# A fused attention and adapter kernel: PSUM as one pool of banks, single-group output, a chosen engine for each eviction, a finer last batch, and a listed order

## The chip, the cores and the metric

One Trainium2 chip, of which the kernel uses one core. The metric is device microseconds (us) of one launch; lower is better.

## The reference

The reference takes q, k and v of shape (8, 8, 576, 64) (batch, heads, sequence, head size) and three weight arrays. It computes attention within a window of 32 positions to each side, joins the 8 heads to rows of 512, and adds to each row a mixture of two of eight rank-16 adapters:

```python
scores = scale * np.matmul(q, k.transpose(0, 1, 3, 2))
mask = np.abs(pos[:, None] - pos[None, :]) <= window          # window = 32
scores = np.where(mask, scores, -1000000000.0)
attn = softmax(scores)                                        # over the last axis
x = np.matmul(attn, v)  ->  rows (4608, 512)
logits = x @ w_gate                                           # 8 experts
topk = np.argpartition(-logits, K, axis=1)[:, :K]             # K = 2
w = softmax of the two chosen logits
delta[mask] += w[mask, k, None] * ((x[mask] @ A[e]) @ B[e])   # for each chosen expert e
return x + delta
```

## The kernel before, in words

The kernel cuts the work into small tasks with two- or three-letter names and numbers. There are 8 batches (b) of 4 units; a unit (u, 0 to 31) is a pair of heads. Queries and keys are loaded as 18 tiles (t) of 128 folded rows; scores are made in 36 tiles (T), two for each t. Each task runs on one engine:

- POOL issues the loads: LD.t.w (line 272; w is 0 for q, 1 for k) and LV.b.o (line 279, v, two halves). It also makes the constants.
- DVE regroups a loaded tile (RG.t.w, line 288), shifts half of v (SV.b.o, line 284), divides the attention output by its row sums (MU.u, lines 355 and 356), evicts transposed rows (XE.b.h, line 374) and computes the gates (G1.b, lines 399 to 404, and G2.b, lines 414 to 420). At the start it clears buffers (ZK, ZV, ZP).
- PE transposes q and k (TR.t.w, line 296, 8 matmuls), makes scores (SC.T, lines 323 and 327, 2 + 8 matmuls), attention times v (PV.u, line 346, 13 matmuls), transposes of the result (TX.b.h, line 368), the projections to adapters and logits (PZ.b, line 382, 20 matmuls), transposes of the gated projections (TZ.b, line 427) and the output (PD.b.h, lines 437 and 440: for each group of 128 rows one matmul of 512 columns for the adapters and four of 128 for the rows themselves).
- ACT evicts transposed keys in two halves (EK.t, line 316), evicts queries for odd t (EQ.t, line 305; even t go to DVE), takes the exponentials (EX.T, line 332) and one small exponential for the gates (GA.b, line 407), and evicts TZ (ZE.b, line 431) and the output (OB.b.h, line 449).
- SP issues the stores (ST.b.h, line 457).

In SBUF a whole tile of q or k is 256 KB, and a half of v for one batch 288 KB. A batch has 5 groups of 128 output rows; h = 0, 1, 2 stands for groups 0 and 1, 2 and 3, and 4.

PSUM is held as three tiles of two banks (W, 1024 float32 columns, for SC, PV, PZ and PD) and two tiles of one bank (T, 1024 float16 columns, for TR, TX and TZ):

```python
Ws = [psum.tile([128, 1024], F32, name=f"W{i}") for i in range(NW)]    # NW = 3
Ts = [psum.tile([128, 1024], F16, name=f"T{i}") for i in range(NTP)]   # NTP = 2
```

The function `plan` sets the order. It gives each task an engine, a cost and a due time, and places the tasks one after the other on engines and PSUM tiles; the kernel then issues them in that order. The order is thus fixed at build time, and each engine works off its own tasks in order. Semaphores between the engines are set by the framework, which looks at what tile each instruction reads and writes.

Of the kernel before, what the change touches and what calls it, by code (L numbers as in the profile page):

```python
# [38 lines left out]
NT = NU * NB // TB  # L39
NV, NPT, NRAW, NCAST, NX, NXT, NOB = 3, 4, 6, 3, 2, 2, 3  # L40
NW, NTP = 3, 2
# [8 lines left out]
class Task:  # L50
    __slots__ = ("key", "eng", "cost", "deps", "take", "give", "due", "start", "end",
                 "left", "users", "ready", "slot", "lat", "seq")

    def __init__(self, key, eng, cost, deps, take=None, give=None, lat=0.2):
        self.key, self.eng, self.cost, self.deps = key, eng, cost, deps
        self.take, self.give, self.lat = take, give, lat


OFF = {"LD": -14.73, "LV": -10.97, "RG": -16.63, "TR": -2.72, "EQ": -37.15, "EK": 25.79, "SV": 12.6,
       "SC": -0.11, "EX": 11.83, "PV": 1.3, "MU": -33.19, "TX": 3.53, "XE": -49.66, "PZ": 7.11,  # L60
       "G1": -57.49, "GA": 7.42, "G2": -66.76, "TZ": -23.09, "ZE": 10.68, "PD": 11.21, "OB": 13.67,
       "ZK": 4.21, "ZV": 30.71, "ZP": 29.46}


def tasks(off=OFF):

    ts = {}

    def add(key, u, eng, cost, deps, take=None, give=None, lat=0.2):
        t = Task(key, eng, cost, deps, take, give, lat)  # L70
        t.due = u + off[key[0]]
        t.seq = len(ts)
        ts[key] = t

    def score_tiles(u):
        return range(NB * u // TB, (NB * u + NB - 1) // TB + 1)

    def units(T):
        return [u for u in range(NU) if T in score_tiles(u)]

    for i in range(NR):
        add(("ZK", i), BT * i / NB - 4, "DVE", 1.25, [])
    for i in range(NPT):
        add(("ZP", i), -3.0 + i, "DVE", 0.56, [])
    for i in range(NV):
        for o in (0, 1):
            add(("ZV", i, o), 4 * i, "ACT" if i == 1 else "DVE", 2.2 if i == 1 else 1.2, [])
    for t in range(NTT):
        u = BT * t / NB
        for w in (0, 1):  # L90
            add(("LD", t, w), u, "DMA", 1.5, [("RG", t - NRAW, w)], lat=2.0)
        for w in (0, 1):
            add(("RG", t, w), u, "DVE", 0.43, [("LD", t, w), ("TR", t - NCAST, w)])
        old = [("SC", 2 * (t - NR) + i) for i in (0, 1, 2)]
        for w in (0, 1):
            add(("TR", t, w), u, "PE", 0.46, [("RG", t, w)] + old, take="T")
        wrap = 0.2 if t % NR in (0, NR - 1) else 0.0
        add(("EQ", t), u, *(("ACT", 1.02 + wrap) if t % 2 else ("DVE", 0.69 + wrap)),
            [("TR", t, 0)], give=("TR", t, 0))
        add(("EK", t), u, "ACT", 2.05, [("TR", t, 1), ("ZK", t % NR)], give=("TR", t, 1))  # L100
    for b in range(B):
        for o in (0, 1):
            add(("LV", b, o), NP * b + o, "DMA", 1.8,
                [("PV", NP * (b - NV) + n) for n in range(NP)], lat=2.0)
            add(("SV", b, o), NP * b, "DVE", 0.78, [("LV", b, o)])
    for T in range(NT):
        t = T // 2
        need = [("EQ", t), ("EK", t)]
        if T % 2 and (TB * T + TB - 1) % NB != NB - 1:
            need.append(("EQ", t + 1))  # L110
        need += [("PV", u) for u in (units(T - NPT) if T >= NPT else [])]
        add(("SC", T), TB * T / NB, "PE", 0.90, need, take="W")
        add(("EX", T), TB * T / NB, "ACT", 1.03, [("SC", T)], give=("SC", T))
    for u in range(NU):
        b = u // NP
        add(("PV", u), u, "PE", 0.80,
            [x for T in score_tiles(u) for x in (("EX", T), ("ZP", T % NPT))]
            + [(k, i, o) for k, i in (("SV", b), ("ZV", b % NV)) for o in (0, 1)]
            + [("TX", b - NX, h) for h in range(3)], take="W")
        add(("MU", u), u, "DVE", 1.05, [("PV", u)], give=("PV", u))  # L120
    off["ST"] = off["OB"]
    for b in range(B):
        v0 = NP * b
# [100 lines left out]
def kernel(  # L224
# [291 lines left out]
    for t in order:  # L516
# [40 lines left out]
```

## Time and profile before

| | |
|---|---|
| time, 3 runs | 145.54, 145.97, 146.17 us (median 145.97) |
| the profiled execution's own time | 147.01 us |
| its span, first to last instruction | 145.0 us |
| PE busy | 119.1 us, 1624 matmuls |
| DVE busy | 109.9 us |
| ACT busy | 111.0 us |
| mean granted TensorE clock | 0.973 |

The profile page has the busy time of each engine, the span in 40 equal slices (a digit is the busy share in tenths; PEclk is the granted clock), the chain of work that ended last, and groups of equal instructions with their mean time and the idle time before them. Other answers of the trace list the waits by pairs of lines, and the instructions in order of time. A row of the chain in order of time reads: start, length, engine, tile, line, count. A row of the timeline reads: start, length, engine, line, operation, output from input, count, and in brackets the idle time before it and what ended it.

### The profile page before, as it was taken

Reading aid. Unit: us, or ns where it says so; the run is one execution under the profiler, and the core shown is the slowest. Engines: PE = TensorE matmul, PEld = TensorE weight load, DVE = VectorE, ACT = ScalarE, POOL = GpSimd, SP = SyncE. Lnnn points to the kernel's source line nnn. Section 1 sums busy time; section 2 is a strip of 40 time slices with the busy share of each in tenths; the row PEclk is TensorE's granted clock in tenths of the full one; section 3 lists DMA queues with packets and bytes.
Section 4 is the critical chain, followed back from the end, with each engine's and each line's share of the span. In section 5 each row is a group of like instructions: output and inputs, shape, how many; then the busy total and the mean of one; then the engine's idle time right before and its main releaser. Section 6 shows DMA issues by size and latency. Waiting matters only on the chain.

```text
span 145.0 us, 4013 instructions
## 1 busy us (share of the span) xinstructions
PE 119.1 (82%) x1624; PEld 100.9 (70%) x1624; DVE 109.9 (76%) x279; ACT 111.0 (77%) x127; POOL 52.0 (36%) x80
## 2 busy tenths in 40 slices
PE   0257959796789599999999999999999999792770
PEld 0246757685677598888979788988898788582440
DVE  5769889993895989899899999989778456946000
ACT  7739877569769569999998999889979975553160
POOL 7998377589534355546256021000000000000000
PEclk9999999999999999999999999999999999999558
DMA  2999999999999999999999999924403050548035
GB/s 10 204 141 183 199 198 188 132 128 142 163 195 180 190 243 207 198 283 229 223 209 276 195 216 280 178 58 156 133 0 127 16 188 5 192 136 300 28 127 199
DMA packets 38770, 24.12 MB, mean 166 GB/s; under 512 B 24800, under 2 KB 34144, under 8 KB 38752
## 3 DMA queue, kind: packets, MB, share of 16 engines
q0 software_dynamic: 33504, 14.43, 84.1%
q1 hardware_dynamic: 5248, 9.44, 19.0%
q8 instruction: 12, 0.20, 0.5%
q14 instruction: 6, 0.05, 0.1%
HBM read 28.85 MB, written 9.44 MB: 264 GB/s over the span
## 4 chain that ended last, share of the span: by engine, by line
PE 51%; DVE 24%; issue 10%; DMA 8%; ACT 2%; POOL 1%; ACTq 0%; DVEq 0%; POOLq 0%
PE W L346 10%; DMA l<-in_q_dram 8%; PE W L323 7%; PE W L327 7%; PE T L296 6%; PE W L437 5%; PE W L382 5%; PE W L440 5%; PE T L368 4%; DVE x L356 4%; DVE c L288 4%; DVE vbd L284 3%; DVE xT L374 3%; DVE rc L355 2%; DVE zs L420 2%
## 5 line engine op out<-in xcount | busy, mean ns | idle before, releaser
L316 ACT COPY kR<-T 64x1024 f16<-64x1024 f16 x36 | 36.2, 1005 | 7.1 <-PE T L296 6.8
L332 ACT ACTIVATE PT<-W 128x1024 f16<-128x1024 f32 x36 | 35.4, 1038 | 5.5 <-PE W L327 4.6
L346 PE MATMUL W<-vbd,PT 128*128 128x130 f16 x416 | 28.6, 219 | 2.0 <-DVE vbd L284 2.0
L296 PE MATMUL T<-ident,c 128*128 128x128 f16 x288 | 22.6, 229 | 9.0 <-DVE c L288 7.7
L449 ACT COPY ob<-W 128x1024 f32<-128x1024 f32 (+1 forms) x24 | 20.9, 876 | 9.9 <-PE W L440 7.7
L356 DVE TENSOR_TENSOR x<-W,rc 128x640 f16<-128x640 f32 x32 | 26.4, 824 | 1.1
L346 PEld LDWEIGHTS <-PT 128*128 128x128 f16 x416 | 25.0, 97 | 2.3 <-DVE vbd L284 2.3
L327 PEld LDWEIGHTS <-kR 128*128 128x128 f16 x288 | 19.5, 99 | 8.9 <-issue 0.7
L296 PEld LDWEIGHTS <-c 128*128 128x128 f16 x288 | 18.7, 103 | 9.7 <-DVE c L288 9.6
L323 PE MATMUL W<-identQ,mask 128*128 128x512 f16 x72 | 22.0, 387 | 2.7 <-DVE x L356 2.7
L327 PE MATMUL W<-qR,kR 128*128 128x128 f16 x288 | 22.4, 222 | 0.0
L272 POOL DMA_DIRECT2D l<-in_k_dram x24 | 15.9, 665 | 10.5 <-DMA l<-in_k_dram 3.1
L279 POOL DMA_DIRECT2D vbd<-in_v_dram x16 | 13.3, 835 | 16.0 <-PE T L427 7.4
L272 POOL DMA_DIRECT2D l<-in_q_dram x24 | 16.4, 683 | 7.0 <-DMA l<-in_k_dram 1.9
L288 DVE COPY c<-l 128x1024 f16<-128x1024 f16 x36 | 14.6, 434 | 5.4 <-DMA l<-in_k_dram 4.5
L440 PEld LDWEIGHTS <-xT 128*128 128x128 f16 x160 | 13.3, 104 | 7.1 <-issue 2.8
L437 PE MATMUL W<-B_sb,zT 128*128 128x512 f16 x40 | 16.4, 410 | 1.8 <-ACT zT L431 0.8
L374 DVE COPY xT<-T 128x1024 f16<-128x1024 f16 (+1 forms) x24 | 13.4, 598 | 4.6 <-PE T L368 3.8
L440 PE MATMUL W<-ident,xT 128*128 128x128 f16 x160 | 16.7, 231 | 0.0
L368 PE MATMUL T<-ident,x 128*128 128x128 f16 x160 | 11.8, 219 | 3.0 <-DVE xT L374 1.5
L284 DVE COPY vbd<-vbd 32x2304 f16<-32x2304 f16 x16 | 12.7, 794 | 0.7 <-DMA vbd<-in_v_dram 0.3
L368 PEld LDWEIGHTS <-x 128*128 128x128 f16 x160 | 9.8, 98 | 3.6 <-DVE x L356 1.7
(49 smaller groups left out, 115.5 us busy)
## 6 DMA issues: line engine op xcount, KB each, us to landing
out_dram<-ob SPq DMA_DIRECT2D x24, 256.0 KB, 2.9
vbd<-in_v_dram POOLq DMA_DIRECT2D x16, 288.0 KB, 9.4
l<-in_q_dram POOLq DMA_DIRECT2D x12, 256.0 KB, 9.6
l<-in_k_dram POOLq DMA_DIRECT2D x12, 256.0 KB, 9.9
out_dram<-ob SPq DMA_DIRECT2D x16, 192.0 KB, 2.9
l<-in_q_dram POOLq DMA_DIRECT2D x4, 192.0 KB, 7.6
l<-in_k_dram POOLq DMA_DIRECT2D x4, 192.0 KB, 7.3
l<-in_q_dram POOLq DMA_DIRECT2D x4, 128.0 KB, 9.1
```

Source lines behind the costliest of these rows:

```text
L272: keep(nc.gpsimd.dma_start(out=raw[w][t % NRAW][f - FT * t:f - FT * t + n], in_=src[f - NF * b:f - NF * b + n]))
L296: keep(nc.tensor.matmul(out=tp[:, FT * slot:FT * slot + FT], lhsT=src[:, j, :], rhs=ident, is_transpose=True, start=True, stop=True))
L316: keep(nc.scalar.copy(out=dst.rearrange("p a (r f j) -> p a r f j", r=2, j=4), in_=kt[64 * o:64 * o + 64]))
L323: keep(nc.tensor.matmul(out=p[:, i:i + 4], lhsT=maskT, rhs=bcast(identQ, 1, 4), start=True, stop=False))
L327: keep(nc.tensor.matmul(out=p[:, i], lhsT=kR[:, a, :], rhs=qR[:, :, 8 * a:8 * a + 16], start=False, stop=(i % 4 == 3)))
L332: keep(nc.scalar.activation(out=PTs[T % NPT][:, :, 64:192].rearrange("p i (f j) -> p i f j", j=J), in_=ps("SC", T).rearrange("p (i j f) -> ...
L346: keep(nc.tensor.matmul(out=po[:, GS * g:GS * g + 2 * VD], lhsT=PTs[T % NPT][:, sl, off:off + 128], rhs=rhs[:, :, V0 - 1:V0 + D], start=(i ...
L356: keep(nc.vector.tensor_tensor(out=xs[b % NX].rearrange("p g (h n d) -> p g h n d", h=2, n=NP)[:, :, :, n], in0=pog[:, :, :, 1:VD], in1=bc ...
L368: keep(nc.tensor.matmul(out=tp[:, c0:c0 + 128], lhsT=xs[b % NX][:, g, 128 * c:128 * c + 128], rhs=ident, is_transpose=True, start=True, st ...
L437: keep(nc.tensor.matmul(out=pd[:, i], lhsT=zTs[b % 2][:, g], rhs=B_sb, start=True, stop=False))
L440: keep(nc.tensor.matmul(out=pd[:, i, 128 * c:128 * c + 128], lhsT=xTs[b % NXT][:, g, c], rhs=ident, start=False, stop=(c == 3)))
L449: keep(nc.scalar.copy(out=dst, in_=src))
```

## The change

- The eight PSUM banks are held as four tiles W0 to W3 of two banks. A task that needs two banks (SC, PV, PZ) takes a tile; a task that needs one takes one half of a tile, which it views as float16 where it holds transposes. The number behind the colon in the list below is the bank: banks 2i and 2i + 1 are the halves of Wi.
- The output is made, evicted and stored by single groups (PD.b.g, OB.b.g, ST.b.g), with 7 buffers of one group instead of 3 of two groups.
- Each eviction has an engine of its own in the list (A for ACT, D for DVE): EK's two halves apart (34 on A, 2 on D), EQ 11 on A and 7 on D, XE 7 on A and 19 on D, OB 30 on A and 10 on D.
- In the last batch TX and XE go by single groups; MU.31 is MA and MB, PZ.7 is PZa and PZb, G2, TZ and ZE have two parts too; and the rows' part of the output (PX) is issued ahead of the gates, and the adapters' part (PB) behind them.
- One comparison of G2 moves into G1. The identity is made ahead of the first load; the mask, the weights' loads and the cleared columns (CQ, CM, WA, WB, Z1) are entries of the list. NRAW goes from 6 to 4, NXT from 2 to 3.
- `Task`, `tasks` and `plan` are gone: the order, the banks and the engines stand in a list.

```diff
-NT = NU * NB // TB
-NV, NPT, NRAW, NCAST, NX, NXT, NOB = 3, 4, 6, 3, 2, 2, 3
-NW, NTP = 3, 2
+NV, NPT, NRAW, NCAST, NX, NXT, NOB = 3, 4, 4, 3, 2, 3, 7
+NW = 4
+LB = B - 1
...
+ORDER = """
+CI ZK.1 LD.0.0 LD.0.1 ZK.2 LD.1.0 ZV.1.0:A ZP.2 LD.1.1 ZP.1 WB ZK.0 ZV.2.0:A CQ RG.0.0 CM
+ZV.0.1:D TR.0.0:0 LV.0.0 RG.0.1 LD.2.0 ZK.3 EQ.0:A TR.0.1:1 RG.1.0 LD.2.1 EK.0.0:A RG.1.1
+TR.1.0:0 Z1.2 Z1.1 ZP.3 EK.0.1:A TR.1.1:2 LD.3.0 EQ.1:D LD.3.1 EK.1.1:A SC.0:4 ZP.0 LV.0.1
+ZV.2.1:D EK.1.0:A LD.4.0 SC.1:0 ZV.0.0:D EX.0 LD.4.1 SC.2:2 RG.2.0 EX.1 RG.2.1 LV.1.0 ZK.4
+TR.2.0:4 EX.2 TR.2.1:5 WA RG.3.0 EQ.2:A Z1.0 ZV.1.1:D TR.3.0:2 EQ.3:A SC.3:0 RG.3.1 SV.0.0
+EK.2.0:A TR.3.1:4 SV.0.1 LV.1.1 EX.3 EK.3.0:D PV.1:2 LD.5.0 EK.2.1:A PV.2:0 LD.5.1 MU.1 EK.3.1:A
+PV.0:6 LD.6.0 MU.2 SC.4:2 LD.6.1 MU.0 SC.5:4 EX.4 SC.6:0 LV.2.0 RG.4.0 EX.5 RG.4.1 LV.2.1 PV.3:2
+SV.1.0 EX.6 TR.4.1:4 LD.7.0 MU.3 TR.4.0:5 LV.3.1 EK.4.1:A TX.0.1:2 LD.7.1 EQ.4:A SV.1.1 TX.0.0:3
+LD.8.0 TX.0.2:0 XE.0.1:D PV.4:6 LD.8.1 XE.0.2:A RG.5.0 LV.3.0 EK.4.0:A SC.7:0 MU.4 LD.9.0
+TR.5.0:2 XE.0.0:D EX.7 PV.5:6 RG.5.1 SC.8:4 EQ.5:A MU.5 LD.9.1 PZ.0:0 EX.8 RG.6.0 RG.6.1 LD.10.0
+TR.5.1:6 G1.0 TR.6.1:7 LD.10.1 EK.5.0:A PV.6:4 SV.2.0 SC.9:2 GA.0 EK.5.1:A G2.0 EX.9 TR.6.0:6
+EQ.6:A MU.6 TZ.0:0 PV.7:2 ZE.0:A RG.7.0 SC.10:4 LV.4.1 MU.7 EK.6.1:A SC.11:0 LD.11.0 SV.3.1
+EX.10 TX.1.0:6 RG.7.1 TX.1.2:2 LV.4.0 TX.1.1:3 EX.11 XE.1.0:D TR.7.1:4 LD.11.1 XE.1.1:D TR.7.0:5
+EK.6.0:A PD.0.1:6 RG.8.0 PD.0.0:3 XE.1.2:D EQ.7:A LD.12.0 SC.12:0 RG.8.1 SV.2.1 LD.12.1 OB.0.1:A
+TR.8.0:2 SV.3.0 EX.12 TR.8.1:5 ST.0.1.1 PV.9:6 EQ.8:D OB.0.0:A PV.8:0 MU.9 EK.8.0:A ST.0.0.0
+PZ.1:2 MU.8 EK.7.1:A SC.13:6 EK.7.0:A G1.1 PV.10:0 EX.13 RG.10.0 PD.0.4:4 MU.10 GA.1 SC.15:6
+OB.0.4:A G2.1 EK.8.1:A ST.0.4.4 PV.11:0 EX.15 PD.0.3:4 LV.5.1 PD.0.2:5 MU.11 TZ.1:2 OB.0.3:A
+LV.5.0 SC.14:6 ZE.1:A RG.9.1 ST.0.3.3 TX.2.2:4 RG.9.0 EX.14 TX.2.1:0 RG.10.1 LD.13.0 TX.2.0:1
+XE.2.1:D TR.9.1:2 XE.2.2:A PV.12:6 XE.2.0:D EK.9.0:A LD.13.1 RG.11.1 TR.9.0:4 MU.12 PD.1.0:3
+OB.0.2:A LD.14.0 PV.13:0 EQ.9:A ST.0.2.2 RG.12.0 LD.14.1 TR.10.1:6 MU.13 TR.10.0:7 OB.1.0:A
+SC.16:4 EK.9.1:A ST.1.0.5 RG.12.1 RG.11.0 PZ.2:0 EX.16 SV.4.1 LD.15.0 EQ.10:D SC.17:2 EK.10.1:A
+LD.15.1 G1.2 PV.14:4 EX.17 PD.1.1:7 LD.16.0 MU.14 OB.1.1:A PV.15:2 LD.16.1 GA.2 ST.1.1.6
+EK.10.0:A PD.1.4:7 G2.2 LV.6.1 SC.19:4 OB.1.4:A LV.6.0 PD.1.2:6 EX.19 ST.1.4.9 PD.1.3:7 MU.15
+TZ.2:0 TR.11.1:1 OB.1.2:A RG.13.0 SC.20:4 ZE.2:A ST.1.2.7 RG.14.1 LD.17.0 OB.1.3:A RG.13.1
+TX.3.2:6 TX.3.0:0 XE.3.2:D EX.20 LD.17.1 ST.1.3.8 TX.3.1:7 XE.3.0:D SC.18:2 EK.11.1:A XE.3.1:D
+TR.11.0:0 SV.4.0 TR.12.0:7 EX.18 TR.12.1:6 RG.15.0 PV.17:4 EQ.11:A EQ.12:D PV.16:2 MU.17
+EK.11.0:A PD.2.4:0 PD.2.0:7 MU.16 OB.2.4:A SC.23:4 EK.12.1:A ST.2.4.14 OB.2.0:D SC.21:0 EX.23
+RG.15.1 ST.2.0.10 PZ.3:2 RG.14.0 SV.5.0 EX.21 SC.22:4 G1.3 EK.12.0:A PV.18:0 SV.5.1 EX.22
+SC.24:6 MU.18 GA.3 PV.19:4 EX.24 G2.3 PD.2.3:0 LV.7.1 TR.13.0:1 OB.2.3:A PD.2.1:6 LV.7.0 EQ.13:A
+TR.13.1:7 ST.2.3.13 MU.19 TZ.3:2 TR.14.0:3 OB.2.1:A SC.25:0 RG.16.1 ZE.3:A ST.2.1.11 EQ.14:D
+EK.13.1:A TX.4.1:6 TX.4.2:2 RG.17.0 TX.4.0:4 XE.4.2:D EX.25 PD.3.0:5 XE.4.0:D PV.20:2 OB.3.0:A
+XE.4.1:D TR.14.1:4 EK.13.0:A ST.3.0.15 MU.20 PD.2.2:5 PV.21:0 OB.2.2:A SV.7.0 PZ.4:6 EK.14.1:A
+ST.2.2.12 MU.21 EK.14.0:A PD.3.1:5 SC.26:2 G1.4 OB.3.1:A PV.22:0 EX.26 ST.3.1.16 RG.16.0 SC.27:4
+RG.17.1 GA.4 MU.22 TR.16.0:2 EX.27 TR.15.0:3 G2.4 PV.23:0 EQ.15:A PD.3.4:4 TR.15.1:5 MU.23
+OB.3.4:A TZ.4:6 PD.3.2:3 EK.15.0:A ST.3.4.19 PD.3.3:4 EQ.16:D TX.5.1:7 OB.3.2:A SV.6.0 TX.5.0:0
+ZE.4:A ST.3.2.17 TX.5.2:1 SC.28:2 XE.5.0:D OB.3.3:A XE.5.2:D EK.15.1:A PD.4.3:6 ST.3.3.18
+XE.5.1:D PD.4.2:4 SC.29:0 EX.28 SV.6.1 OB.4.2:D TR.16.1:7 EX.29 PV.24:2 SV.7.1 ST.4.2.22 PZ.5:4
+EK.16.0:A MU.24 EK.16.1:A PV.25:0 G1.5 SC.30:2 OB.4.3:A MU.25 ST.4.3.23 GA.5 SC.31:6 EX.30 G2.5
+TR.17.0:0 EX.31 PV.26:2 TR.17.1:1 MU.26 TZ.5:4 EK.17.0:A PV.27:6 EQ.17:D PD.4.4:5 ZE.5:A SC.32:2
+MU.27 PD.5.0:4 EX.32 OB.4.4:D TX.6.2:0 TX.6.0:6 XE.6.2:D TX.6.1:7 ST.4.4.24 XE.6.0:A OB.5.0:D
+SC.33:2 EK.17.1:D ST.5.0.25 XE.6.1:A PV.28:4 PD.4.1:0 EX.33 MU.28 PZ.6:6 OB.4.1:A PV.29:4 G1.6
+ST.4.1.21 SC.34:0 MU.29 GA.6 SC.35:2 EX.34 G2.6 PD.4.0:4 EX.35 PV.30:0 PD.5.1:5 OB.4.0:A MU.30
+PV.31:2 OB.5.1:A ST.4.0.20 TZ.6:4 ST.5.1.26 MA.31 PD.5.4:5 ZE.6:A PD.5.3:0 MB.31 TX.7.0:1
+TX.7.1:4 OB.5.3:D XE.7.0:A TX.7.4:2 TX.7.2:3 TX.7.3:6 XE.7.1:D XE.7.2:A PD.6.0:7 ST.5.3.28
+XE.7.4:D PD.6.1:4 XE.7.3:A OB.5.4:D PZa.7:2 OB.6.1:A ST.5.4.29 PZb.7 OB.6.0:A ST.6.1.31 PD.6.2:4
+G1.7 ST.6.0.30 PD.5.2:5 OB.6.2:A PX.7.0:6 ST.6.2.32 PD.6.3:4 OB.5.2:D GA.7 PX.7.1:0 G2a.7
+ST.5.2.27 G2b.7 TZa.7:5 OB.6.3:D ZEa.7:A TZb.7:2 ZEb.7:A PB.7.0 ST.6.3.33 PB.7.1 OB.7.0:A
+OB.7.1:D PX.7.2:2 PB.7.2 OB.7.2:A ST.7.0.99 OB.7.3:A ST.7.1.99 OB.7.4:D ST.7.2.99 ST.7.3.99
+ST.7.4.99 PD.6.4:2 OB.6.4:A ST.6.4.34
+"""
...
-    ts, order = plan()
+    order, where = [], {}
+    for word in ORDER.split():
...
     def ps(*key):
-        t = ts[key]
-        return (Ws if t.take == "W" else Ts)[t.slot]
+        return Ws[int(where[key]) // 2]
+
+    def bank(*key):
+        i = int(where[key])
+        return Ws[i // 2][:, 512 * (i % 2):512 * (i % 2) + 512]
+
+    def bank16(*key):
+        return bank(*key).bitcast(F16)
+
+    def copy_on(*key):
+        return nc.scalar.copy if where[key] == "A" else nc.vector.tensor_copy
...
+    def MA(u):
+        recip(u)
+        mult(u, 0, 3)
+
+    def MB(u):
+        mult(u, 3, NG)
...
+    def gs(b, h):
+        return range(h, h + 1) if b == LB else range(2 * h, min(NG, 2 * h + 2))
...
+    def resid(b, g, pd, first):
+        for c in range(4):
+            keep(nc.tensor.matmul(out=pd[:, 128 * c:128 * c + 128], lhsT=xTs[b % NXT][:, g, c],
+                                  rhs=ident, start=(first and c == 0),
+                                  stop=(not first and c == 3)))
+
+    def PD(b, g):
+        delta(b, g, bank("PD", b, g), start=True, stop=False)
+        resid(b, g, bank("PD", b, g), False)
...
+    def PX(b, h):
+        for g in range(2 * h, min(NG, 2 * h + 2)):
+            resid(b, g, half(b, g), True)
+
+    def PB(b, h):
+        for g in range(2 * h, min(NG, 2 * h + 2)):
+            delta(b, g, half(b, g), start=False, stop=True)
+
+    def OB(b, g):
+        src = half(b, g) if b == LB else bank("PD", b, g)
+        keep(copy_on("OB", b, g)(out=obs[(NG * b + g) % NOB], in_=src))
...
```

365 lines of the change are left out of this document (112 added, 253 removed).

## The prediction

> **What bounds the kernel now.** I read the page's slices first, then the chain in order of time, then the timeline of the two ends and the groups of equal instructions.
>
> ```profile
> span 145.0 us, 4013 instructions
> PE   0257959796789599999999999999999999792770
> DVE  5769889993895989899899999989778456946000
> ACT  7739877569769569999998999889979975553160
> PEclk9999999999999999999999999999999999999558
> GB/s 10 204 141 183 199 198 188 132 128 142 163 195 180 190 243 207 198 283 229 223 209 276 195 216 280 178 58 156 133 0 127 16 188 5 192 136 300 28 127 199
> ```
>
> PE is full from slice 14 (51 us) to slice 34 (127 us). Ahead of that it has holes, behind it holes and half the clock. DVE and ACT are not far behind PE in the middle. What one task costs PE at full clock stands in the chain, where the starts follow each other without a hole:
>
> ```profile
> 65.40 0.43 PE W L323 x2
> 65.83 0.45 PE W L327 x8
> 66.28 0.45 PE T L296 x8
> 66.73 1.18 PE W L382 x20
> 67.91 0.75 PE W L346 x13
> ...
> 74.70 0.28 PE T L427 x5
> ...
> 88.13 0.89 PE T L368 x16
> ...
> 89.90 0.23 PE T L368 x4
> ...
> 108.12 0.22 PE W L440 x4
> 108.56 0.22 PE W L440 x4
> ```
>
> So SC is 0.88, TR 0.45, PZ 1.18, PV 0.75, TZ 0.28, TX of a batch 1.12, and an output group 0.44 (from one start to the next). All of it: 36 x 0.45 + 36 x 0.88 + 32 x 0.75 + 8 x (1.12 + 1.18 + 0.28) + 40 x 0.44 = 110.1 us. The span is 35 us longer: that is the head, the tail, and little else. Three places on the timeline cut it up:
>
> ```profile
> 5.81 0.77 PEld L296 LDWEIGHTS <-c 128*128 128x128 f16 x8 [5.81 <-DVE c L288]
> 12.42 1.06 PE L323 MATMUL W<-identQ,mask 128*128 128x512 f16 x2
> 18.87 0.81 DVE L284 COPY vbd<-vbd 32x2304 f16<-32x2304 f16 x1
> 19.74 1.67 PE L346 MATMUL W<-vbd,PT 128*128 128x130 f16 x26 [1.79 <-DVE vbd L284]
> 28.54 0.59 PE L323 MATMUL W<-identQ,mask 128*128 128x512 f16 x2
> 36.52 0.59 PE L323 MATMUL W<-identQ,mask 128*128 128x512 f16 x2 [1.64 <-DVE x L356]
> 49.22 0.91 PE L346 MATMUL W<-vbd,PT 128*128 128x130 f16 x13
> 124.19 0.91 PE L346 MATMUL W<-vbd,PT 128*128 128x130 f16 x13
> 131.20 0.20 DVE L399 TENSOR_REDUCE m<-W 128x5 f32<-128x40 f32 x1 [1.64 <-PE W L382]
> 133.54 0.82 DVE L420 TENSOR_TENSOR zs<-W,gate 128x640 f16<-128x640 f32 x1
> 134.43 0.71 PE L427 MATMUL T<-ident,zs 128*128 128x128 f16 x5 [2.82 <-DVE zs L420]
> 139.60 1.50 ACT L449 COPY ob<-W 128x1024 f32<-128x1024 f32 x2 [0.69 <-PE W L440]
> ```
>
> The row at 49.22 is PV.8. Counted along PE's instructions, 15 TR, 13 SC, 9 PV, two TX, one PZ, one TZ and two output groups are done at its end (49.97): 29.5 us of work, 20.5 lost. The row at 124.19 is PV.31, the last; behind it stand 11 output groups, two TZ, one TX and one PZ, 7.7 us. Between the two, 110.1 - 29.5 - 7.7 = 72.9 us of work take 75.1 us: the middle loses 2.2. The tail takes 145.0 - 125.1 = 19.9 us.
>
> **The change: what each edit costs its engine.**
>
> ```profile
> L316 ACT COPY kR<-T 64x1024 f16<-64x1024 f16 x36 | 36.2, 1005 | 7.1 <-PE T L296 6.8
> L332 ACT ACTIVATE PT<-W 128x1024 f16<-128x1024 f32 x36 | 35.4, 1038 | 5.5 <-PE W L327 4.6 <-DVE rc L355 0.7
> L356 DVE TENSOR_TENSOR x<-W,rc 128x640 f16<-128x640 f32 x32 | 26.4, 824 | 1.1
> L288 DVE COPY c<-l 128x1024 f16<-128x1024 f16 x36 | 14.6, 434 | 5.4 <-DMA l<-in_k_dram 4.5 <-DMA l<-in_q_dram 0.7
> L449 ACT COPY ob<-W 128x1024 f32<-128x1024 f32 x16 | 16.3, 1016 | 8.5 <-PE W L440 6.3 <-issue 1.1 <-ACT kR L316 0.8
> L374 DVE COPY xT<-T 128x1024 f16<-128x1024 f16 x16 | 10.5, 688 | 4.1 <-PE T L368 3.4 <-ACT ob L449 0.5
> L305 ACT COPY qR<-T 128x1024 f16<-128x1024 f16 x9 | 9.1, 1014 | 2.6 <-PE T L296 2.4
> L431 ACT COPY zT<-T 128x640 f16<-128x640 f16 x8 | 5.6, 695 | 2.7 <-PE T L427 2.6
> L449 ACT COPY ob<-W 128x512 f32<-128x512 f32 x8 | 4.8, 596 | 1.4 <-PE W L440 1.3
> ```
>
> Single groups: 40 copies instead of 24. Thirty on ACT are 30 x 0.596 = 17.9 us where 16.3 + 4.8 = 21.1 were; ten go to DVE. A 512-column float32 copy on DVE is in no row: between 0.34 (half of the 688 ns, float16) and 0.82 (640 columns of float32); I take 0.65, from the nearer float32 row. DVE gets 6.5 us. ACT in turn gets two more EQ (2 us), five large-batch XE and two small (5 us) and loses two EK. So ACT and DVE each carry some 3 to 5 us more in all; PE's 110.1 us stay. SP issues 40 stores as before, and the store buffers hold slightly more: nothing. NRAW from 6 to 4 costs nothing as long as a tile is regrouped 10 us before the tile four later is needed; in the walk below RG.8.0 frees its buffer at 46 for a tile used at 62.
>
> **The change: the waits.** The built program shows what the list doesn't say. Bank numbers are free, but the semaphores are set by tile, and a tile is now a pair of banks that different tasks hold. Two places, in the order of the built program:
>
> ```
> PE   18 L189 Matmult W_103<-ident,c_0_84 128x128 [waits Activation_49]
> DVE 274 L414 TensorCopy ob_97<-W_106 128x512 [waits DMAHW4_49,Activation_49]
> ```
>
> The first is TR.0.1 into bank 1: it waits for ACT's copies of EQ.0 out of bank 0. The second is OB.7.1 on DVE, which waits for OB.7.0 on ACT, two reads of different banks. Some hundred instructions wait like this, among them PE in front of nearly every single output group, and ACT and DVE for each other. So I walked the list by hand, each engine in its order, with the durations above, these waits, and 0.05 us for a semaphore.
>
> ```profile
> 3.51 0.23 POOL masks.py:197 MEMSET ident<- 128x128 f16 x1
> 3.81 0.29 POOL masks.py:199 TENSOR_SCALAR_AFFINE_SELECT ident<-ident 128x128 f16<-128x128 f16 x1
> ```
>
> *Head.* The identity is made ahead of the first load (these two rows, some 0.6 us), so TR.0.0 starts at 6.4. EQ.0 ends at 8.65, and only then TR.0.1 may start; EK.0.0 ends at 10.75, TR.1.0 (bank 0) at 11.8, EK.0.1 (bank 1) behind it at 12.85. SC.0 starts at 12.9, before at 12.42. The second half of v for batch 0 is now loaded behind tile 3: 2.8 MB instead of 2.1 MB. Before, its shift began at 18.87 and PV at 19.74; the 0.7 MB more take 3.6 us at the 198 GB/s of slice 6. If the loads came strictly one after the other, it would land near 18.8 even so (the first five slices, 18.1 us, moved 2.7 MB). I take 21.5, nearer to the first since that is counted from a landing, and PV starts at 22.3. In between PE has scores and transposes of tiles 2 and 3 to do, and bank pairs give room for three scores at once: SC.6 is done at 28 (before it began at 28.54 and took 0.88). From there DMA, DVE and these waits carry it to the end of SC.12 at 47.9. The same set of tasks was done before at 49.97 - 0.75 (PV.8) + 0.45 (TR.7.1) = 49.7. **Head: -1.8 us.**
>
> *Middle.* Up to PV.31 the list now has 101.5 us of PE work (13 output groups come behind it, before 11), less 29.2 done, that is 72.3. In the walk PE stops here: for an OB or EK of the other bank, or a chain through one, in front of PZ.1 (0.6), PD.0.4 and PD.0.3 (0.4), PD.1.1 and PD.1.4 (1.45), TX.3.2 and TX.3.1 (0.65), TR.11.0 (0.5), TX.4.1 (1.4), TR.14.1 (0.7), PD.3.1 (0.85), PD.3.3 (0.95) and PD.4.2 (0.3), in all 7.8; for other work in front of SC.15, PV.15 and PD.2.3, 1.6; small change 0.9. That is 10.3 us where 2.2 were lost. PV.31 ends at 47.9 + 72.3 + 10.3 = 130.5, before 125.1. Against the head's gain that is **middle: +7.2 us** (0.6 less work, 8.1 more waiting, rounded with the steps).
>
> A typical step: EQ.14 (DVE, bank 3) waits for ZE.3 (ACT, bank 2), EK.13.1 stands behind ZE.3 on ACT, TX.4.1 (bank 6) waits for EK.13.1 (bank 7) and PE stands still from 90.3 to 91.7.
>
> *Tail.* From the end of PV.31: MA 0.85 and MB 0.45, by columns from the 824 ns; five TX and five XE, the XE in turn on ACT and DVE, done at +4.4; PZa and PZb at +5.5; the gates' first part at +6.8 (both parts took from 131.20 to 134.4 before, and take as long in themselves). OB.5.2 (DVE) stands ahead of the second part and waits for PD.6.3 in the other bank, so the second part starts at +8.1 and ends at +10.2; TZa and ZEa, behind OB.6.3, at +11.4; PB and the last five OB up to +14.3. From the last copy's end to the end of the span it is 145.0 - 141.1 = 3.9 us as before. In all 18.2 instead of 19.9. **Tail: -1.7 us.** What helps is that the rows' part of the output no longer stands behind the gates: before, ten matmul steps at half the clock followed ZE.
>
> On the clock: PE idles 2.0 us behind PX in the walk. In the trace 2.82 us idle were followed by five transposes in 0.71 instead of 0.28; a shorter idle than that, of 1.64 us, was followed by full speed. Between the two I take full clock; at half it is up to 1.3 us more. The Trainium skill, "TensorE: Matmul & The Clock Gate", Part 1, has the clock fall after an idle window of about 3.4 us; by that nothing is added here, though the measured fall came after less.
>
> **Sum.** 145.0 - 1.8 + 7.2 - 1.7 = 148.7 us of span; with the 2.0 us around it 150.7 against the profiled 147.01. That execution lies 1.0 above the median of the runs; on the median the same 3.7 us give 149.6. I say 149.5 us.
>
> **Rivals.** *The pair waits bite little: faster.* Most of the middle's stops are shorter than one eviction (0.6 to 1.0 us); if the evictions come up on their queues one place earlier than in the walk, they vanish. With waits by bank alone, the middle loses 3 instead of 10.3, the head gains 3.5 (then the loads of tiles 7 and 8, at 44 to 47 us, end last), the tail 4.9 (OB.5.2, OB.6.3 and OB.7.1 wait no more) and 0.9 of output work moves behind PV.31 into holes: 145.97 - 3.5 + 0.2 - 4.9 = 138. For it: PSUM by banks would let two tasks share a pair. Against it: the waits stand in the built program. The Trainium skill, "PSUM — Partial Sum Buffer", PSUM bank collisions, asks only that two engines keep apart by bank and quadrant; by that rule none of the pair waits is needed by the chip, and the time would be this rival's. It decides if the middle's loss stays below 5 us. Chance 0.23.
>
> *Half the price: level.* The middle at +3.6 instead of +7.2 eats the ends' 3.5: 146. Chance 0.11.
>
> *DVE becomes the bound: slower yet.* DVE's middle, by the rows, is 23 MU, 21 RG, six gates, 12 XE, ten SV, seven EQ or EK and four OB, some 70 us beside PE's 72.3, and it now waits for ACT and is waited for. If it, not PE, ends last through the middle, add 3 us: 152.6. For it: DVE was at nine tenths in most middle slices. Against: before, it ended few waits of PE there. Chance 0.16.
>
> *The change does not do what it says* is part of the forecast: the banks are pooled by number, not in the waits.
>
> **How the numbers follow.** The forecast (slower by 2 to 6 us) has 0.50. What a measurement can tell from no change is about 0.5%, 0.7 us. Faster: 0.23 and 0.02 from the level case, 0.25. Same: 0.07 of the level case. Slower: the rest, 0.68. The likeliest case alone spans 147.5 to 152. The range for all reaches down to 141 (the upper part of the faster rival) and up to 154 (DVE as bound with the half clock in the tail).
>
> **What would show it.** Right: waits of PE for lines 208 and 414 (EK, OB) of half a microsecond and more in the middle, in front of lines 388, 189 and 278; SC.0 near 13 us; the end of PV.31 (last matmul of line 238) near 130; a tail near 18. Wrong: PE full from 40 us on with PV.31 near 118, or SC.12 done before 45. If the middle is as lossy as said and the time is still lower, the tail or the head was mis-sized.

## The result and the profile after

The changed kernel takes 153.3 us (median of 4 runs, 152.66 to 153.88), the kernel before beside it 145.75 us (4 runs, 145.33 to 146.17): 1.052 times as long, 95% interval 1.046 to 1.057. The forecast was 149.5 us, in a range of 141 to 154. The direction is right, and the size is half of what was measured: 3.5 us forecast, 7.5 measured. The profiled execution took 153.19 us. Where some runs of a kernel lie more than 1.5% above its fastest, the median without these upper runs is given below beside the median of all, and the ratios to the kernel before always leave them out.

The page's span and slices:

```profile
span 151.4 us, 4024 instructions
PE   0239648989798899997899987879799999886560
DVE  6876889988995988998577994788699897856430
ACT  8658785898898699987987967877888685662250
PEclk9999999999999999999999999999999999999555
```

PE, full before from 51 to 123 us, now has sevens and eights all through the middle, while DVE and ACT are no fuller. PE and ACT work hardly more (120.6 us for 119.1, 111.9 for 111.0), DVE 6.6 us more (116.5 for 109.9), and everybody waits more. At the end the granted clock is at half for three slices. The timeline has the marks that the forecast named, and some of the stops it listed:

```profile
8.88 1.01 PE L189 MATMUL W<-ident,c 128*128 128x128 f16 x8 [1.19 <-ACT qR L200]
12.65 1.06 PE L215 MATMUL W<-identQ,mask 128*128 128x512 f16 x2
48.21 0.61 PE L219 MATMUL W<-qR,kR 128*128 128x128 f16 x8
92.68 1.28 PE L278 MATMUL W<-ident,x 128*128 128x128 f16 x20 [1.08 <-ACT kR L208]
95.79 0.61 PE L189 MATMUL W<-ident,c 128*128 128x128 f16 x8 [0.65 <-ACT ob L414]
99.56 0.38 PE L388 MATMUL W<-B_sb,zT 128*128 128x512 f16 x1 [0.79 <-ACT kR L208]
106.81 0.38 PE L388 MATMUL W<-B_sb,zT 128*128 128x512 f16 x1 [0.90 <-ACT kR L208]
129.83 0.91 PE L238 MATMUL W<-vbd,PT 128*128 128x130 f16 x13
```

The first row is TR.0.1, which waits until ACT has emptied the other bank of its pair; SC.0 follows at 12.65. SC.12 is done at 48.7 (start of its last eight matmuls plus 0.45), PV.31 at 130.7. Called head up to the end of SC.12, middle up to the end of PV.31, and tail behind it, the head is 1.0 us shorter than before (48.7 for 49.7), the middle 6.6 longer (82.0 for 75.4), the tail 0.8 longer (20.7 for 19.9): 6.4 us, the difference of the spans. The four rows between are TX.4.1, TR.14.1, PD.3.1 and PD.3.3. Each waits for an EK or OB (lines 208, 414) in the other bank. The waits by pairs of lines have them together:

```profile
PE W L388 <- ACT kR L208: 3.2, 5, 0.9
PE W L189 <- ACT kR L208: 3.0, 4, 1.1
PE W L189 <- ACT qR L200: 1.2, 1, 1.2
PE W L278 <- ACT kR L208: 1.1, 1, 1.1
```

(Columns: microseconds in all, times, longest.) The copies themselves cost what was assumed; the ones on DVE took 0.689 us where 0.65 was guessed:

```profile
L414 ACT COPY ob<-W 128x512 f32<-128x512 f32 x30 | 17.3, 588 | 11.5 <-PE W L392 4.1 <-DVE xT L284 1.5 <-PE W L189 1.3
L414 DVE COPY ob<-W 128x512 f32<-128x512 f32 x10 | 6.9, 689 | 5.7 <-ACT ob L414 2.3 <-PE W L392 1.2 <-ACT kR L208 0.8
```

The tail, from the timeline:

```profile
138.60 0.69 DVE L414 COPY ob<-W 128x512 f32<-128x512 f32 x1 [0.98 <-PE W L392]
140.79 0.72 PE L362 MATMUL W<-ident,zs 128*128 128x128 f16 x5 [1.78 <-DVE zs L343]
142.11 0.75 ACT L366 COPY zT<-W 128x384 f16<-128x384 f16 x2 [4.08 <-DVE ob L414]
142.64 1.89 PE L388 MATMUL W<-B_sb,zT 128*128 128x512 f16 x4 [1.13 <-ACT zT L366]
144.33 0.69 DVE L414 COPY ob<-W 128x512 f32<-128x512 f32 x1 [2.31 <-ACT ob L414]
146.16 0.58 PE L388 MATMUL W<-B_sb,zT 128*128 128x512 f16 x1 [0.78 <-DVE ob L414]
147.21 0.58 ACT L414 COPY ob<-W 128x512 f32<-128x512 f32 x1 [1.53 <-PE W L392]
```

OB.5.2 on DVE (138.60) waits for PE (PD.6.3 in the other bank) and holds the gates' second part. PE stands for 1.78 us, and its five transposes then make a row of 0.72 us, where such a row is 0.44 long at full clock (TZ.6, at 131.15). ZEa waits for OB.6.3 on DVE in the other bank, and OB.7.1 for OB.7.0 in the other bank. PD.6.4 waits for OB.7.4, but that is no pair wait: both use bank 2.

### The profile page after: what moved, and what is told of

Its sections match the earlier page's. It is cut to its first block, busy times and chain, and to the rows that moved or that the text cites. A ratio compares the mean times of both kernels' runs of the same rounds, so it can differ in the third digit from the quotient of the medians.

```text
span 151.4 us, 4024 instructions
## 1 busy us (share of the span) xinstructions
PE 120.6 (80%) x1624; PEld 100.6 (66%) x1624; DVE 116.5 (77%) x284; ACT 111.9 (74%) x143; POOL 53.5 (35%) x80
## 4 chain that ended last, share of the span: by engine, by line
PE 28%; ACT 11%; DVE 9%; issue 4%; ACTq 0%; DVEq 0%
PE W L388 6%; ACT kR L208 5%; PE W L238 5%; PE W L392 4%; PE W L189 3%; ACT ob L414 3%; DVE ob L414 3%; PE W L219 3%; PE W L215 3%; PE W L294 2%; ACT zT L366 2%; PE W L278 2%; DVE xT L284 1%; ACT xT L284 1%; PE W L362 1%
## 5 line engine op out<-in xcount | busy, mean ns | idle before, releaser
L208 ACT COPY kR<-W 64x1024 f16<-64x1024 f16 x34 | 34.0, 1006 | 7.3 <-PE W L189 4.2
L189 PE MATMUL W<-ident,c 128*128 128x128 f16 x288 | 22.1, 229 | 13.7 <-DVE c L181 8.8
L255 DVE TENSOR_TENSOR x<-W,rc 128x640 f16<-128x640 f32 (+2 forms) x33 | 26.5, 804 | 1.3 <-DVE rc L248 0.2
L414 ACT COPY ob<-W 128x512 f32<-128x512 f32 x30 | 17.3, 588 | 11.5 <-PE W L392 4.1
L172 POOL DMA_DIRECT2D vbd<-in_v_dram x16 | 14.3, 898 | 23.9 <-PE W L238 13.6
L392 PEld LDWEIGHTS <-xT 128*128 128x128 f16 x160 | 12.2, 99 | 11.2 <-issue 7.1
L181 DVE COPY c<-l 128x1024 f16<-128x1024 f16 x36 | 16.3, 474 | 1.8 <-PE W L189 1.6
L284 DVE COPY xT<-W 128x1024 f16<-128x1024 f16 (+1 forms) x19 | 10.8, 589 | 7.5 <-PE W L278 3.9
L392 PE MATMUL W<-ident,xT 128*128 128x128 f16 x160 | 15.3, 223 | 0.0
L198 ACT COPY qR<-W 128x1024 f16<-128x1024 f16 x11 | 11.1, 1012 | 3.2 <-PE W L189 3.1
L177 DVE COPY vbd<-vbd 32x2304 f16<-32x2304 f16 x16 | 12.2, 765 | 1.4 <-DMA vbd<-in_v_dram 0.9
L278 PE MATMUL W<-ident,x 128*128 128x128 f16 x160 | 10.6, 219 | 2.3 <-ACT kR L208 1.1
```

Of the source, the lines that this page charges most:

```text
L181: keep(nc.vector.tensor_copy(out=cst[w][t % NCAST], in_=raw[w][t % NRAW].rearrange("p o (j d) -> p j o d", j=J)))
L189: keep(nc.tensor.matmul(out=tp[:, FT * slot:FT * slot + FT], lhsT=src[:, j, :], rhs=ident, is_transpose=True, start=True, stop=True))
L208: keep(copy_on("EK", t, o)(out=dst.rearrange("p a (r f j) -> p a r f j", r=2, j=4), in_=kt[64 * o:64 * o + 64]))
L255: keep(nc.vector.tensor_tensor(out=xg[:, g0:g1, :, n], in0=pog[:, :, :, 1:VD], in1=bcast(rcs[u][:, g0:g1], 3, D), op=ALU.mult))
L392: keep(nc.tensor.matmul(out=pd[:, 128 * c:128 * c + 128], lhsT=xTs[b % NXT][:, g, c], rhs=ident, start=(first and c == 0), stop=(not first ...
L414: keep(copy_on("OB", b, g)(out=obs[(NG * b + g) % NOB], in_=src))
```

## The experiments

**One tile of eight banks.** The same list, banks and engines; the framework then sets its waits by bank, since the pairs are no tiles any more.

```diff
-    Ws = [psum.tile([128, 1024], F32, name=f"W{i}") for i in range(NW)]
+    WW = psum.tile([128, 1024 * NW], F32, name="WW")
+    Ws = [WW[:, 1024 * i:1024 * i + 1024] for i in range(NW)]
```

> Same list, same banks, same engines; the eight banks are slices of one tile, so that the built program waits by bank instead of by pair. Theory (the pair waits are the price of the change): the stops of PE in front of lines 189, 278 and 388 behind an EQ, EK or OB of the other bank go, the middle (SC.12 to PV.31) loses about 3 us instead of 10, the tail some 4 us less, and the kernel takes 138 us (136 to 141), below both kernels. Rival 1 (the list's own order and its even split between ACT and DVE are the price): 150 us or more. Rival 2 (half and half): 144 to 147.

143.48 us (141.42 to 145.14, 4 runs; 141.9 from two runs without the upper ones), with 146.26 for the kernel before beside it (lowest of 13 runs 145.19): below both kernels, 9.8 us below the changed one (11.4 without the upper runs). Its waits by pairs of lines, its timeline, and its groups:

```profile
PE WW L389 <- DVE ob L415: 0.8, 1, 0.8
```

```profile
47.46 0.61 PE L220 MATMUL WW<-qR,kR 128*128 128x128 f16 x8
121.85 0.91 PE L239 MATMUL WW<-vbd,PT 128*128 128x130 f16 x13
```

```profile
L415 ACT COPY ob<-WW 128x512 f32<-128x512 f32 x30 | 17.3, 589 | 3.5 <-PE WW L393 2.6 <-ACT qR L201 0.4 <-PE WW L389 0.2
```

Of their waits for EK and OB, 4.0 us before, the output matmuls (now line 389) keep a single one, 0.8 us: PD.6.4 behind OB.7.4, in one and the same bank. SC.12 is done at 47.9, PV.31 at 122.8, and the span ends at 139.5: the middle takes 74.9 us instead of 82.0, the tail 16.7 instead of 20.7. The same 30 copies wait 3.5 us in all instead of 11.5. The pair waits are the price of the change; this is shown. But the time is 5.5 us above the expected 138 (3.9 without the upper runs), so something else ends the waits now.

**The same for the kernel before.**

```diff
-    Ws = [psum.tile([128, 1024], F32, name=f"W{i}") for i in range(NW)]
-    Ts = [psum.tile([128, 1024], F16, name=f"T{i}") for i in range(NTP)]
+    WW = psum.tile([128, 512 * (2 * NW + NTP)], F32, name="WW")
+    Ws = [WW[:, 1024 * i:1024 * i + 1024] for i in range(NW)]
+    Ts = [WW[:, 1024 * NW + 512 * i:1024 * NW + 512 * i + 512].bitcast(F16)
+          for i in range(NTP)]
```

> The kernel before, with its PSUM buffers as slices of one tile in the same way. Theory: it takes its banks in whole tiles and evicts pairs of groups together, so it has hardly any wait across banks to lose; only the eight single groups of its last batch do. 145 to 146 us, no change. Rival (one tile by itself is faster, whatever the list): 2 us or more below the kernel before.

146.77 us (10 runs) beside 146.26; ratio to the kernel before 1.001 (0.997 to 1.005). One tile by itself brings nothing; it brings 9.8 us to a list that shares pairs.

**Work for TensorE in the tail's idle time.** Four tiles; between G2b and TZa stands PF, 20 transposes of the identity into the unused half of TZa's bank (its code is left out here):

```diff
-ST.5.2.27 G2b.7 TZa.7:5 OB.6.3:D ZEa.7:A ...
+ST.5.2.27 G2b.7 PF.7:5 TZa.7:5 OB.6.3:D ZEa.7:A ...
```

> The changed kernel with 20 transposes of the identity added in front of TZa (line 362), into the unused part of its bank, in the 1.8 us in which TensorE otherwise stands. Theory (the tail came out 2.6 us longer than forecast since the clock fell to half there): the transposes of TZa take 0.28 us instead of 0.72, the four deltas 0.88 instead of 1.89, and the end comes 1.0 to 1.4 us earlier: 152 us. Rival (the copies of ACT and DVE set the end, whatever the clock): below 0.4 us, 153 us.

153.59 us, ratio to the kernel before 1.048 (1.041 to 1.055): the time doesn't show a gain. The timeline does:

```profile
131.39 0.91 PE L238 MATMUL W<-vbd,PT 128*128 128x130 f16 x13
142.35 0.62 PE L362 MATMUL W<-ident,zs 128*128 128x128 f16 x5 [0.17 <-DVE zs L343]
144.04 1.04 PE L393 MATMUL W<-B_sb,zT 128*128 128x512 f16 x4 [1.08 <-ACT zT L366]
147.28 0.59 ACT L419 COPY ob<-W 128x512 f32<-128x512 f32 x1 [1.03 <-PE W L397]
```

The four deltas (PB.7.0 and PB.7.1) take 1.04 instead of 1.89 us, and the last copy ends 15.6 us behind PV.31 instead of 17.05: 1.5 us for the clock, as the theory said. The row of the five transposes is 0.62 us, not 0.28. But from the last copy's end to the end of the span it is now 4.4 us instead of 3.6, so the tail is only 0.7 us shorter (20.0 for 20.7). The head of this execution is 1.5 us longer than in the changed kernel's (SC.12 is done at 50.2), so no gain is left in its time; that the same holds for the median is likely and not shown.

**OB.5.2 and OB.6.3 on ACT.**

```diff
-... PD.6.3:4 OB.5.2:D GA.7 PX.7.1:0 G2a.7 ST.5.2.27 G2b.7 TZa.7:5 OB.6.3:D ZEa.7:A ...
+... PD.6.3:4 GA.7 OB.5.2:A PX.7.1:0 G2a.7 ST.5.2.27 OB.6.3:A G2b.7 TZa.7:5 ZEa.7:A ...
```

> The changed kernel with OB.5.2 and OB.6.3 on ACT behind GA, instead of on DVE ahead of the gates' second part and of ZEa. Theory (DVE's two copies, one late by a wait for the other bank, hold the gates and then ZEa): the gates' second part begins at +7.4 us behind PV.31 instead of +8.6, ZEa loses its 0.5 us of waiting, TensorE's idle time falls to 0.7 us and the clock stays up: 2 to 3 us less, 150.5 us. Rival (the clock falls all the same, or the two copies on ACT hold ZEa instead): 1 us less at most, 152.5 us.

150.72 us (150.45 without the one upper run), ratio 1.029 (1.024 to 1.034), 2.6 us less. The profiled execution is that upper run and took 153.22; what it lost lies ahead of SC.12, which is done at 51.2 (the last section has the row), and only its tail is read:

```profile
132.35 0.91 PE L238 MATMUL W<-vbd,PT 128*128 128x130 f16 x13
140.58 0.17 DVE L336 TENSOR_SCALAR s<-dm 128x5 f32<-128x5 f32 x1 [0.43 <-ACT dm L330]
142.30 0.49 PE L362 MATMUL W<-ident,zs 128*128 128x128 f16 x5 [0.76 <-ACT ob L414]
143.20 1.04 PE L388 MATMUL W<-B_sb,zT 128*128 128x512 f16 x4 [0.41 <-ACT zT L366]
```

The second part of the gates begins at +7.3 behind PV.31 instead of +8.5, PE stands 0.76 us instead of 1.78, the clock stays up until TensorE is done, and the tail takes 151.5 - 133.3 = 18.2 us. That this is the forecast's figure is a coincidence: the forecast had the two copies on DVE. In the three other executions the mean granted clock is 0.992 to 0.997, so it stayed up there too; in the four of the changed kernel it is 0.965 to 0.970.

**The engines of the evictions.** 19 letters of the list: every OB and EK on A, every XE on D; once with one tile, once with four.

> The one-tile kernel with a fixed engine for three kinds of eviction, as in the kernel before: OB, EK on ACT, XE on DVE (19 letters of the list). By the rows ACT gets 10 x 0.585 + 2 x 1.0 and loses 5 x 1.0 + 2 x 0.58, 1.7 us more; DVE 4.6 us less. Theory (the choice of engine serves the order of the list: a copy goes to the queue that is free): 1 to 3 us above the one-tile kernel, 145 to 146.5 us. Rival (with the pair waits gone the choice is worth nothing): 143 to 144 us.

144.3 us (10 runs; 143.7 without the upper ones), ratio 0.984 (0.979 to 0.989). That is 0.8 above the one-tile kernel by all runs, and 1.8 above it without the upper ones, of which the one-tile kernel has only two left. So theory (1 to 3 us) and rival (nothing) stay undecided: the choice of engines is worth some 0 to 2 us.

> The changed kernel, four tiles, with the same fixed engines (OB, EK on ACT, XE on DVE). Theory (the price is the wait for the other bank of a pair, whoever empties it; TensorE waits for it all the same): 152.5 to 154.5 us. Rival (the price is that evictions of one pair stand on two engines, which now wait for each other): 150 us or less.

153.82 us, ratio 1.056 (1.045 to 1.067): as expected, 0.5 from the changed kernel. With four tiles it doesn't matter to the time whose copy it is; that PE waits for the other bank does.

**What holds the one-tile kernel.** Three experiments on its loads. Two leave out the loads of 12 k tiles, in the one-tile kernel and in the changed one; the third has six load buffers instead of four.

```diff
-... LD.6.1 ... LD.17.1 ...       # first two: words LD.t.1 with t >= 6 taken out of the list
-NRAW = 4
+NRAW = 6                         # third
```

> The one-tile kernel without the loads of the k tiles 6 to 17 (they are regrouped from what the buffers hold; all other work stays): 3.1 MB of 14.4 less, 15.7 us less of loading at 196 GB/s. Theory (without the pair waits the loads are what the one-tile kernel waits for up to 80 us, and why its runs lie between 141.4 and 145.1): 138 to 140 us, with runs close together. Rival (the engines' own work and order bound it): 142.5 to 143.5 us, as scattered as before.

140.86 us (140.4 to 141.96), ratio 0.965 (0.957 to 0.974).

> The changed kernel, four tiles, without the same loads. Theory (the pair waits bound it, the loads come early enough behind its head): 1 us at most below the changed kernel, 152 to 153.5 us. Rival (the loads bound it too): 149 us or less.

153.71 us, ratio 1.052 (1.040 to 1.063).

> The one-tile kernel with six load buffers a side, as in the kernel before, instead of four. Theory (the loads run without a gap up to 80 us already, so more buffers bring none of them sooner): 142.5 to 144 us, no change. Rival (four buffers hold the loads back): 141.5 us or less.

143.6 us (141.29 to 145.9; 141.7 without the upper runs). So the loads cost the changed kernel nothing. They cost the one-tile kernel 2.6 us on the median of all runs and 1.0 without the upper ones, and buffers don't change that. 140.86 is a little above the expected 138 to 140: the loads are part of what is missing to 138, not all. What they do above all is to make executions differ. The four runs without these loads lie within 1.6 us, those of the one-tile kernel within 3.7. In seven traces with one tile the middle takes 74.3 to 75.3 us in the four where DVE waits at most 0.96 us at a time for a k tile, and 77.1 to 79.6 in the three where it waits 2.8 to 3.3 us for one.

**Where v's second half is loaded.**

```diff
-LV.0.0 RG.0.1 LD.2.0 ... SC.0:4 ZP.0 LV.0.1
+LV.0.0 LV.0.1 RG.0.1 LD.2.0 ... SC.0:4 ZP.0
```

> The one-tile kernel with the second half of v for batch 0 loaded right behind the first half (ahead of tile 2) instead of behind tile 3. Theory (the head is bound by the sum of the loads; TensorE waits 10.7 us for regrouped tiles and only 1.6 us for v): PV.1 starts up to 1.5 us earlier, tiles 2 and 3 come 1.5 us later (0.3 MB at 198 GB/s), no gain: 143.5 to 145 us. Rival (the late half of v is what the head lost against the forecast, by its wait and the half clock behind it): 1.5 us or more below the one-tile kernel, 142 us.

144.0 us (142.1 to 145.97; 142.1 without the upper runs), no gain. But the theory's step didn't show: PV.1 starts at 23.3 instead of 22.6, later and not earlier, and the second transpose of tile 3 at 21.2 instead of 20.4. That the head is bound by the sum of its loads fits, and isn't shown.

**The one-tile kernel with another tail.** As in the tail experiment, and PD.6.4 ahead of TZa.

```diff
-... OB.5.2:D GA.7 ... G2b.7 TZa.7:5 OB.6.3:D ... OB.7.0:A OB.7.1:D ... ST.7.4.99 PD.6.4:2 OB.6.4:A ST.6.4.34
+... GA.7 OB.5.2:A ... OB.6.3:A PD.6.4:4 G2b.7 TZa.7:5 ... OB.7.0:A OB.6.4:D ST.6.4.34 OB.7.1:D ... ST.7.4.99
```

> The one-tile kernel, tail alone changed: OB.5.2 and OB.6.3 on ACT behind GA, and the last group of batch 6 (PD.6.4) ahead of TZa in bank 4 instead of behind OB.7.4 in bank 2, its copy on DVE. Theory (in the one-tile kernel the last copy is OB.6.4 at 134.4, since PD.6.4 waited 0.8 us for OB.7.4): the last copy is OB.7.4, 1.3 us earlier, and the gates' second part 0.3 us earlier: 1.2 to 1.8 us below the one-tile kernel, 142 us. Rival (the stores' landing sets the end): 0.5 us or less, 143 us.

142.72 us (142.04 to 144.01), ratio 0.980 (0.971 to 0.989): 0.8 below the one-tile kernel by all runs, 0.8 above it without the upper ones. A gain in the time isn't shown, which is nearer to the rival.

```profile
73.17 0.76 DVE L182 COPY c<-l 128x1024 f16<-128x1024 f16 x2 [3.14 <-DMA l<-in_k_dram]
124.99 0.91 PE L239 MATMUL WW<-vbd,PT 128*128 128x130 f16 x13
134.54 1.93 DVE L415 COPY ob<-WW 128x512 f32<-128x512 f32 x3 [0.97 <-ACT zT L367]
```

The last copy ends at 136.5, 10.6 us behind PV.31 (12.2 without the edit), but the span ends 5.7 us later (142.2) instead of 4.5. Of the 1.6 us gained up to the last copy 0.4 are left in the tail (16.3 us for 16.7). The first row is the loads again: DVE waits 3.14 us for a k tile; in the one-tile kernel's trace the same wait was 0.96 us. This execution is the slowest of the four, and its middle takes 78.9 us for 74.9, though no edit touches it.

**Both, and work for TensorE in the head.** The last kernel with 26 transposes between TR.3.1 and PV.1.

> The one-tile kernel with the other tail, and 26 transposes of the identity into a free bank between TR.3.1 and PV.1, where TensorE stood idle for 1.5 us. In some traces so far the 39 matmuls of the first three PV behind that idle time took 2.4 us, in others 3.9 to 4.0. Theory (those are executions in which the clock fell in the idle time; with work in it it cannot): 2.4 us for the 39, and on the mean some 0.5 to 1 us below the one-tile kernel with the other tail (142.7), 142 us, with the upper runs gone. Rival (the late loads of later tiles take up what the head gains): 142.5 to 143.5 us, as scattered.

146.28 us (12 runs; 145.34 without the upper ones), ratio 0.994 (0.989 to 0.999): 3.6 us above the same kernel without the 26 transposes, 2.6 without the upper runs. A miss.

```profile
22.64 2.42 PE L239 MATMUL WW<-vbd,PT 128*128 128x130 f16 x39 [0.16 <-DVE vbd L178]
73.16 0.76 DVE L182 COPY c<-l 128x1024 f16<-128x1024 f16 x2 [3.33 <-DMA l<-in_k_dram]
136.76 1.89 DVE L420 COPY ob<-WW 128x512 f32<-128x512 f32 x3 [2.95 <-DMA out_dram<-ob]
```

The head did what was wanted: the first three PV at full clock. Then the k tile comes no earlier, and at the end OB.6.4 waits 2.95 us on DVE for its buffer, which the store of OB.5.2 still holds; OB.7.1 and OB.7.4 stand behind it. The edit of the tail made that wait possible, and in the trace above it didn't show. In this trace the tail takes 18.3 us where it took 16.3, PV.31 ends 0.2 us later than there, and the span is 2.2 us longer, near the 2.6 of the runs. Why the buffer comes later here stays open.

## Why the prediction was right in direction and wrong in size

- **The pair waits**, read off the built program, were the mechanism, and in the middle their price was right: +6.6 us for a forecast of +7.2, and five traces with four tiles have the middle at 81.8 to 82.1 us. Four of its longer stops agree: 1.08 for 1.4 at TX.4.1, 0.65 for 0.7 at TR.14.1, 0.79 for 0.85 at PD.3.1, 0.90 for 0.95 at PD.3.3. Others came out smaller: PD.1.1 and PD.1.4 have 0.56 for 1.45, TX.3.2 and TX.3.1 0.39 for 0.65. Taking the waits away alone gives 9.8 us back.
- **The head** is -1.0 us for -1.8 in the profiled execution. That it comes so near is in part luck: in the four other traces with four tiles the clock fell to half during the first three PV, and SC.12 is done at 50.2 to 51.2 us instead of 48.7, later than the 49.7 of before. So the sum of head and middle, +5.6 for +5.4, holds for an execution in which the clock stays up there.
- **The tail is the term that was mis-sized**: -1.7 forecast, +0.8 measured, 2.5 us. The steps hold up to the end of the gates (+10.2 forecast, +10.3 measured). The steps behind it failed: ZE ends at +12.1 instead of +11.4, the last copy at +17.05 instead of +14.3. The first choice that failed is the one on the clock: between a stop of 1.64 us with full speed and one of 2.82 with half, full clock was taken for 2.0 us; the stop was 1.78 us and the clock fell. The length of a stop couldn't tell: in the kernel before one of 1.79 us has full speed behind it (the row at 19.74), and the last section has what goes with the fall. It was priced at up to 1.3 us and costs 1.5 to the last copy, of which 0.7 reaches the end of the span (the experiment with work in the idle time). The other 1.3 us to the last copy are there at full clock too: in that experiment ZE ends at +12.0 and the last copy at +15.6. (The span ends 3.6 us behind the last copy instead of 3.9, which takes 0.3 off.) The trace shows the copies waiting for each other behind the gates (ZEa behind OB.6.3, OB.7.1 behind OB.7.0, and PD.6.4 behind OB.7.4 in its own bank); which of these steps the walk had too short isn't on record. With OB.5.2 and OB.6.3 on ACT the time falls by 2.6 us.
- **The last step of the sum failed too**: 1.0 us was taken off since the profiled execution of before lay that much above its median. The walk gave absolute times, and the changed kernel's profiled execution lies at its median (153.19 and 153.3). 150.7 should have stood. The two together, 2.5 and 1.0, with +0.8 and -0.6 in head and middle, are the 3.8 us between 149.5 and 153.3 (0.1 from rounding). Two slips of the working change nothing: the middle has 0.9 us less work and not 0.6 (8.1 - 0.9 is the 7.2 that stands there), and PE was full up to slice 33 (123 us), not 34.
- **The faster rival** has the right mechanism for the one-tile kernel and too high a price: 138 against 143.5 (141.9 without the upper runs). It gave 3.5 us for the head, 0.2 of loss for the middle, 4.9 for the tail; the one-tile trace shows 1.8, a gain of 0.5, and 3.2. The loads, which it named for the head only, reach into the middle (DVE's wait for a k tile). The Trainium skill, "PSUM — Partial Sum Buffer", PSUM bank collisions, asks engines to keep apart by bank and quadrant only; the trace agrees: in the one-tile kernel, where ACT and DVE copy out of both halves of a pair at once (OB.7.0 from 131.89, OB.7.1 from 132.10), the copies take 589 and 686 ns on average, with pair waits 588 and 689.
- **DVE as the bound** names nearly the right number (152.6) for the wrong reason: DVE is busy 77% of the span, and PE's added waits are mostly for ACT's copies.
- **NRAW from 6 to 4 at nothing** was right as far as tried: in the one-tile kernel six buffers change nothing.

## What to carry to other kernels

When banks are pooled by number, look in the built program at what a wait is set on: a pool whose tiles are larger than what a task holds has the tasks wait for each other, and a list that was made without these waits pays for them in every stop; slices of one tile gave 9.8 us back here. Carry a walk's absolute time to the end, and correct it by the offset of the old kernel's profile only if something says that the new one shares it. A tail is a chain of small steps: walk it copy by copy with each engine's queue, and take the clock's worse case where PE works less than half of some 3.4 us, however short the single stops are.

## What the runs showed of the hardware

The clock's fall doesn't follow the length of one idle stretch. The first three PV (39 matmuls), in the changed kernel, the one with work in the tail's idle time, the one with OB.5.2 and OB.6.3 on ACT, the one-tile kernel and the one-tile kernel with fixed engines:

```profile
23.60 2.40 PE L238 MATMUL W<-vbd,PT 128*128 128x130 f16 x39 [0.63 <-DVE vbd L177]
```

```profile
23.58 4.01 PE L238 MATMUL W<-vbd,PT 128*128 128x130 f16 x39 [0.64 <-DVE vbd L177]
```

```profile
24.58 3.96 PE L238 MATMUL W<-vbd,PT 128*128 128x130 f16 x39 [1.19 <-DVE vbd L177]
```

```profile
22.59 3.90 PE L239 MATMUL WW<-vbd,PT 128*128 128x130 f16 x39 [1.61 <-DVE vbd L178]
```

```profile
23.04 2.42 PE L239 MATMUL WW<-vbd,PT 128*128 128x130 f16 x39 [1.61 <-DVE vbd L178]
```

An idle time of 1.61 us was followed by 1.5 us more for the same work in one execution and not in another, and so was one of 0.63 or 0.64. What goes with the fall can be read from the traces. In all fourteen the granted clock, from its first rise on, changes only at whole multiples of 3.41 us, and these intervals lie at another place in each execution. It fell at the end of every interval in which PE was busy for 1.44 us or less, at none with 1.71 or more, and between the two it did either (510 intervals in all). The intervals around the last two rows, with PE's busy time (and its matmuls), the granted clock, and the share and GB/s of the DMA, first in the one-tile kernel, then with fixed engines:

```profile
18.97:22.38 3.41, 1.39 (x18) 1.00 1.50 190
22.38:25.80 3.42, 3.21 (x30) 0.50 5.17 103
```

```profile
18.44:21.86 3.42, 2.00 (x26) 1.00 1.40 194
21.86:25.27 3.41, 2.23 (x39) 1.00 5.32 102
```

In the changed kernel's tail the interval from 137.35 to 140.76 has 1.44 us of work, and the clock is at half behind it. The Trainium skill, "TensorE: Matmul & The Clock Gate", Part 1, speaks of an idle window of about 3.4 us; the length agrees with these traces, but the interval need not be idle: 1.65 us of work in it was still followed by the fall once. Part of the head's scatter from one execution to the next, 1.5 us, comes with it.

The end of the span comes 3.3 to 5.8 us behind the last copy, more when the last copies lie close together: 3.6 in the changed kernel, 5.7 in the one-tile kernel with the other tail. In the two experiments that shortened the tail up to the last copy by 1.5 and 1.6 us, 0.7 and 0.4 us of it were left at the end of the span.
